# A linear-attention recurrence with a gated MLP: the cyclic timetable worked out anew, loads of the inner dense products twelve positions ahead

## The chip, the cores and the metric

The kernel runs on one core of a Trainium2 chip. The metric is device time in microseconds of one execution, from the core's own run. Three runs of the kernel before took 732.81, 734.06 and 735.11 us; the median is 734.06 us. The profiled execution, on which all rows below rest, took 736.0 us, of which 733.8 us lie between its first and last instruction.

## The reference

A recurrence over 768 time steps, for 4 batches and 8 heads of 40 values each, is followed by an MLP with spatial gating over the result. The code below is shortened; all of it is float32.

```
# attention: state is [B, H, 40, 40]
for t in range(768):
    y[t]  = einsum('bhd,bhde->bhe', r[t], state)
    Sa    = einsum('bhde,bhe->bhd', state, a[t])
    state = state * w[t][:, :, None, :] - einsum('bhd,bhe->bhde', Sa, b[t])
    state = state + einsum('bhd,bhe->bhde', v[t], k[t])
x = y as [4, 768, 320]
# MLP
h = gelu_tanh(x @ w_in)                       # 320 -> 1024
u, v = h[..., :512], h[..., 512:]
v_n  = (v - mean(v)) / sqrt(var(v) + 1e-6) * g_ln
v_s  = einsum('ts,bsd->btd', w_sg, v_n) + b_sg[None, :, None]
out  = x + (u * v_s) @ w_out                  # 512 -> 320
```

## The kernel before, in words

**Chunks.** The 768 steps are cut into 12 chunks of 64 (`C`, `NCH`), and each chunk into two halves f = 0 and f = 1 of two batches each. Within a chunk the recurrence becomes dense products; between chunks only the state is carried.

**Three kinds of work for a chunk.** (1) *Gates* (`gate_1` to `gate_n`, L303 to L378): scans over the decays on VectorE, products `ab` and transposes `kt` on TensorE; they need the tile `main` (642 KB a half chunk in two DMAs, two buffers) and run about four chunks ahead. (2) *Inverse* (`inv_sub`, L383): a triangular inverse for two chunks at a time, as 58 multiply and add instructions on GpSimd (POOL, tiles `tg` and `x`), turned by VectorE (`x1z`) and completed by the small products `gp` and `xp`. (3) *Chain* (`chain1` L464 to `post5` L585): the recurrence itself. For each half: `ru`, `us`, `ut`, `sp`, `pq`, `yp` on TensorE, and each one's result is taken out by ScalarE (`rhsb`, `vu`, `vut`) or VectorE (`pqs`, `yt`); `sp` gives the new state, copied to `vs` for the next chunk's `ru`; `tp` turns the state for `yp`, and ScalarE copies it to `s2` (shown as `s`; two buffers, L493). `post5` stores the half chunk's result `yt` to `xd` in DRAM, in four DMAs.

**Inner dense products ("fills").** While the recurrence runs, the first 640 of the 768 tokens of every batch are already taken through half of `x @ w_in`. There are 20 such fills, one for a batch and 128 tokens: `fill_x` loads `xf` from `xd` (three DMAs, L880), `fill_split` makes the rounded part `xfh` on ScalarE (L887), `fill_low` makes the rest `xfl` on POOL and stores both (L894), `fill_v` multiplies (`hf`, eight products, L904), `fill_out` copies `hf` to `hv` on ScalarE and stores it to `hd` (L912; `hv` has one buffer). The weights for this come in six stages `wstep` (L1044): load `stg`, ScalarE `size`, VectorE steps, ScalarE `wvh`, and a last step on VectorE, or on POOL in stages 1, 3 and 5. After the recurrence `run` (L1074) does the rest of the MLP.

**What sets the order.** There is no scheduler. Each piece of work is put into a list with a *position*, a number worked out by hand from tables (L42 to L88): `PER` is the number of positions from one chunk to the next, `YC` the position at which a chunk's chain begins, `GATE`, `CHAIN`, `FILL`, `INV`, `BACK` give each piece's distance from it. `in_order` (L98) sorts the list and holds pieces back where a PSUM bank is still taken in that order. Every instruction, DMAs too, is then issued in this order on its engine: all DMAs on one queue (SP), which stops at a DMA whose tile isn't free or whose source isn't there, with all later ones behind it. The code gives a position no unit.

**Lines that matter here.** The load of the next `main` stands in `gate_3`, straight behind the last reader (L333); the loads for the chain follow their last reader by 0.001 positions:

```
if i == 1:
    load_main(2 * c + f + 2)                                  # L333
at_(z + n[0] + 0.001, load_vb, c + 1, f)                      # L627
at_(z + max(n[6], n[9]) + 0.001, load_vu, c + 1, f)           # L628
at_(z + n[13] + 0.001, load_rv, c + 1, f)                     # L629
at(YC[min(2 * k + 2 + b // 2, NCH - 1)] + FEXTRA.get((b, k), 0) + p, f, b, k)   # L1050, fills
```

All instructions are issued by one helper (L172), so the profile shows that line for each, and the tiles' names tell them apart.

Of the kernel before, what the change touches and what calls it, by code (L numbers as in the profile page):

```python
# [18 lines left out]
NCH = S // C  # L19
# [17 lines left out]
WARM = 14  # L37
WARMS = ((-6.677, 8), (-6.177, 8))
BLANKS = -21.0
ZEROS = -36.0  # L40
LOADS = -24.0
PER = 26.5  # L42
GATE = ((-105.675, -104.069, -102.527, -98.826, -101.029, -97.64, -92.831, -91.094, -94.751, -92.741, -92.857),
    (-95.861, -93.341, -91.539, -89.807, -90.663, -89.233, -81.947, -80.028, -86.574, -83.227, -84.708))
CHAIN = ((0.0, 1.572, -9.235, -7.206, 2.08, 2.941, 4.523, 6.296, 11.564, 3.945, 4.686, 5.697, 7.113, 8.443, 10.749),
    (0.973, 2.583, 12.51, 15.829, 3.295, 5.224, 16.164, 18.719, 20.203, 6.977, 8.552, 10.046, 11.456, 17.819, 20.766))
YC = (0, 27.5, 80.0, 106.5, 133.0, 159.5, 186.0, 212.5, 239.0, 265.5, 292.0, 318.5)
YG = (39.675, 59.675, 80.0, 106.5, 133.0, 159.5, 186.0, 212.5, 239.0, 265.5, 292.0, 318.5)
YI = (-5.677, 21.823, 80.0, 133.0, 186.0, 239.0, 292.0)
GATEE = {(0, 0): "VG", (0, 1): "GG"}  # L50
GROUPS = ((0,), (1,), (2, 3), (4, 5), (6, 7), (8, 9), (10, 11))
LAST = 2
NBANK = 6
INV = (-63.232, -55.232, -53.032, 0.764, -8.432, -6.979)
INV1 = (-44.0, -29.3, -27.1, 0.429, -2.0, -1.3)
BACK = (-4.894, -2.14, -3.644, -5.677, -3.145, -1.402, 0.525)
END_GT = 238.772
END_IW = 285.071
END_RING = 286.366
END_IV = 319.525  # L60
CG = 0.7978845608028654
G1 = 0.044715
PIN = 238.782
DSTEP = ((-8.5, -1.0, 0.0, 0.7, 1.4, 2.4), (-8.5, -1.0, 0.0, 0.7, 1.4, 2.4))
DSTEPF = (-2.5, -0.5, 0.0, 0.7, 1.4, 2.4)
DEC = (5.0, 15.0, 25.0, 35.0, 45.0, 55.0, 247.782, 253.782, 259.782, 265.782, 271.782, 277.782)
GE = "VV"
FILL = ((-14.041, -8.441, -7.991, -4.381, -1.035), (3.788, 9.388, 9.838, 14.139, 17.326))
FEXTRA = {}
FILLG = True  # L70
LASTF = 5
PX = 319.725
PXS = 319.735
PV = 286.466
PS = 336.549
PL = 329.549
PF = (310.0, 315.0, 320.0, 325.0, 330.0)
PH = 9
# [7 lines left out]
SGS = (5, 3, 5, 6, 7, 8, 8, 11, 10, 11, 12, 11)  # L86
PO = 238.792
DECO = (283.782, 289.782, 295.782, 301.782, 307.782, 313.782, 319.782, 325.782)  # L88
DSTEPO = (-8.5, -1.0, 0.0, 0.7, 1.4, 2.4)
# [8 lines left out]
def in_order(pieces):  # L98
# [7 lines left out]
    def emit(x):  # L106
        nm = x[1].__name__
        if nm in USES and not (nm == "chain_t" and x[2][0] == 0 or nm == "chain3" and x[2][0] == NCH - 1):
            n, _, k = USES[nm]
            if any(left[b] for b in banks[max(0, len(banks) - NBANK):max(0, len(banks) + n - NBANK)]):  # L110
                return False
            left[key(x)] = k
            banks.extend([key(x)] * n)
        for r, n in ends:
            if nm == r and key(x, n) in left:
                left[key(x, n)] -= 1
        out.append(x)
        return True

    def behind(x):  # L120
# [3 lines left out]
        for h in held:  # L124
            hn = h[1].__name__
            if (nm, hn) in ends and key(x, hn) == key(h) or nm == "copy3" and hn == "post3" and x[2] == h[2]:
                return True
            if nm == "gate_3" and hn.startswith("gate") or nm.startswith("load_v") and hn.startswith("chain"):
                return True
# [56 lines left out]
def attention(tc, a, xd, flag, keep, ps, mlp=None):  # L186
# [4 lines left out]
    with ExitStack() as ctx:  # L191
# [32 lines left out]
        n = WU  # L224
# [78 lines left out]

        gate, kbs, unit, x1_of, st2, pqt, bk, xin = {}, {}, {}, {}, {}, {}, {}, {}

# [17 lines left out]
        def gate_3(c, f, i, E=V):  # L323
# [7 lines left out]
            E.tensor_tensor(out=kbs[c, f][:, i].rearrange("p q x t -> p x q t"), in0=kab[:, i, 0:3:2], in1=hv, op=ALU.mult)  # L331
            if i == 1:
                load_main(2 * c + f + 2)  # L333

# [275 lines left out]
        for c in range(NCH):  # L610
            for f in range(2):
# [9 lines left out]
                for h in range(2):  # L621
                    at_(y + n[9] + 0.001 * h, gate_a, c, f, h)
                    at_(y + n[10] + 0.001 * h, gate_n, c, f, h)
                z, n = YC[c], CHAIN[f]
                for g, p in zip((chain1, post1, chain_t, post_t, chain2, post2, chain3, post3, copy3, chain_u, post_u, chain4, post4, chain5, post5), n):
                    at_(z + p, g, c, f)
                at_(z + n[0] + 0.001, load_vb, c + 1, f)  # L627
                at_(z + max(n[6], n[9]) + 0.001, load_vu, c + 1, f)  # L628
                at_(z + n[13] + 0.001, load_rv, c + 1, f)  # L629
            z = YC[c]  # L630
# [44 lines left out]
class Mlp:  # L675
# [354 lines left out]
    def side(self):  # L1030
# [216 lines left out]
```

## Time and profile before

| | |
|---|---|
| median of three runs | 734.06 us |
| profiled execution | 736.0 us (span 733.8 us) |
| granted TensorE clock, mean | 0.841 |
| TensorE busy (products / weight loads) | 578.4 us (79%) / 525.2 us (72%) |
| VectorE, ScalarE, GpSimd busy | 485.6, 334.2, 354.3 us |
| DMA | 89.5 MB, mean 122 GB/s |
| first `ru` of chunks 0, 1, 2, 11 | 70.83, 109.30, 181.35, 473.6 us |
| last `yt` of the recurrence begins | 506.3 us |

The program has three stretches: gates and inverse of the first chunks until 70.8 us, the recurrence with its fills to about 507 us, and the MLP's rest. In the chunk-to-chunk stretch the chunk's start is read from the first product `ru` of half 0. A position and a microsecond can be compared there: from chunk 2 to chunk 11 the tables count 9 x 26.5 = 238.5 positions, and the profile 292.28 us.

### The profile page before, as it was taken

The numbers are of one execution on the slowest core, as the hardware profiler recorded it, in microseconds if no ns is written. First come the engines' busy times: TensorE is split into PE (matmuls) and PEld (weight loads), VectorE is DVE, ScalarE is ACT, GpSimd is POOL, SyncE is SP. The second block draws the span as 40 slices with busy tenths as digits, with TensorE's granted clock in tenths as the row PEclk, the third lists the DMA queues.
The fourth block names the chain that finished last, engine by engine and source line by source line (L and its number), as shares of the span: only waits on it lengthen the run. The fifth ranks groups of instructions, "written<-read, shape, count | busy, mean of one in ns | idle before, by whom it ended". The sixth has DMA issues, their size and how long they took to land.

```text
span 733.8 us, 25290 instructions
## 1 busy us (share of the span) xinstructions
PE 578.4 (79%) x10710; PEld 525.2 (72%) x10710; DVE 485.6 (66%) x950; ACT 334.2 (46%) x736; POOL 354.3 (48%) x596
## 2 busy tenths in 40 slices
PE   5474746626879799888987789759789998899996
PEld 4463646625768698777875578558679997799995
DVE  5864765876647674776758764345648979978942
ACT  2342444444555646466564645453424523444410
POOL 4386722785474358347836944123433423424331
PEclk8577866756889967799998877859899999999999
DMA  5470352533444645556455353654532275142001
GB/s 182 131 158 22 92 126 63 136 76 99 128 125 123 189 116 147 147 153 179 113 165 148 107 147 109 166 177 133 158 128 71 76 253 157 53 169 71 28 22 38
DMA packets 87138, 89.50 MB, mean 122 GB/s; under 512 B 38280, under 2 KB 69000, under 8 KB 85000
## 3 DMA queue, kind: packets, MB, share of 16 engines
q1 hardware_dynamic: 87016, 87.79, 42.2%
q8 instruction: 86, 1.41, 0.8%
q14 instruction: 36, 0.29, 0.1%
HBM read 68.10 MB, written 19.66 MB: 120 GB/s over the span
## 4 chain that ended last, share of the span: by engine, by line
PE 30%; DVE 18%; DMA 14%; ACT 7%; issue 6%; POOL 6%; SPq 4%; POOLq 0%; ACTq 0%; DVEq 0%
PE sg L172 8%; SPq L172 4%; PE ut L172 3%; PE yp L172 3%; PE op L172 3%; DVE v L172 3%; PE hf L172 2%; PE pq L172 2%; DVE p L172 2%; DMA hd<-hv 2%; POOL x L172 2%; DMA xf<-xd 2%; PE sp L172 2%; DVE g L172 2%; DMA rt<-rt 2%
## 5 line engine op out<-in xcount | busy, mean ns | idle before, releaser
L172 POOL TENSOR_TENSOR tg<-x,n 128x135 f32<-128x135 f32 (+25 forms) x203 | 104.5, 515 | 55.6 <-issue 15.5
L172 POOL TENSOR_TENSOR x<-x,tg 128x135 f32<-128x135 f32 (+25 forms) x203 | 108.7, 535 | 15.8
L172 PE MATMUL ab<-at,kb 64*64 64x64 f32 x1536 | 39.4, 261 | 48.8 <-DVE kb L172 20.9
L172 ACT ACTIVATE nts<-ab 32x512 f32<-32x512 f32 x96 | 46.5, 484 | 60.4 <-PE ab L172 59.2
L172 PEld LDWEIGHTS ab<-at,kb 64*64 64x64 f32 x1536 | 34.6, 172 | 53.8 <-DVE kb L172 23.7
L172 PE MATMUL sg<-wsl,vh 128*128 128x384 f32 x192 | 67.9, 354 | 5.5 <-POOL wsl L172 3.6
L172 PE MATMUL sg<-wsh,vh 128*128 128x384 f32 x192 | 67.6, 352 | 5.6 <-ACT wsh L172 3.3
L172 POOL TENSOR_TENSOR gx<-g,gy 128x384 fp32r<-128x384 f32 x32 | 34.1, 1070 | 74.0 <-ACT gy L172 74.0
L172 PE MATMUL sg<-wsh,vl 128*128 128x384 f32 x192 | 67.7, 352 | 0.9 <-POOL vl L172 0.9
L172 POOL TENSOR_TENSOR xfl<-xf,xfh 128x256 fp32r<-128x256 f32 x20 | 15.1, 757 | 83.8 <-ACT xfh L172 80.9
L172 POOL TENSOR_TENSOR rs<-rs,mhalf 128x1 f32<-128x1 f32 x24 | 14.9, 625 | 78.7 <-DVE rs L172 75.0
L172 DVE TENSOR_TENSOR at<-ab,mask 64x512 f32<-64x512 f32 x48 | 32.1, 677 | 27.8 <-ACT nts L172 18.2
L172 ACT CAST gy<-g 128x384 fp32r<-128x384 f32 x32 | 16.4, 513 | 62.9 <-DVE g L172 60.7
L172 PEld LDWEIGHTS sg<-wsl,vh 128*128 128x128 f32 x192 | 37.8, 197 | 7.7 <-POOL wsl L172 4.4
L172 PE MATMUL ut<-ident,vu 64*64 64x64 f32 x768 | 40.8, 257 | 2.6 <-ACT vu L172 2.2
L172 PEld LDWEIGHTS sg<-wsh,vh 128*128 128x128 f32 x192 | 38.0, 198 | 6.6 <-ACT wsh L172 3.9
L172 ACT CAST vh<-v 128x512 fp32r<-128x512 f32 x24 | 14.6, 619 | 60.3 <-DVE v L172 60.3
L172 PE MATMUL yp<-pqs,kbt 128*64 128x64 f32 x768 | 35.5, 253 | 8.0 <-DVE pqs L172 7.5
L172 PE MATMUL pq<-rt,vut 40*64 40x64 f32 x1536 | 38.5, 263 | 3.7 <-ACT vut L172 2.3
L172 PE MATMUL gp<-x1z,nts 64*32 64x32 f32 x768 | 18.2, 212 | 28.1 <-DVE x1z L172 27.2
L172 PEld LDWEIGHTS ut<-ident,vu 64*64 64x64 f32 x768 | 35.0, 167 | 6.5 <-ACT vu L172 3.5
L172 PEld LDWEIGHTS yp<-pqs,kbt 128*64 128x64 f32 x768 | 30.5, 162 | 12.7 <-DVE pqs L172 9.9
(154 smaller groups left out, 1589.3 us busy)
## 6 DMA issues: line engine op xcount, KB each, us to landing
main<-main SPq DMA_DIRECT2D x44, 321.4 KB
hd<-hv SPq DMA_DIRECT2D x20, 256.0 KB
v<-hd SPq DMA_DIRECT2D x20, 256.0 KB
vu<-vs SPq DMA_DIRECT2D x24, 160.0 KB
vs<-vb SPq DMA_DIRECT2D x24, 160.0 KB
rt<-rt SPq DMA_DIRECT2D x48, 80.0 KB
vut<-vt SPq DMA_DIRECT2D x48, 80.0 KB
xd<-yt SPq DMA_DIRECT2D x96, 40.0 KB
```

Source lines behind the costliest of these rows:

```text
L172: return self.tc.keep_in_program_order(f(*a, **k))
```

## The change

The tables are replaced. `PER` falls from 26.5 to 25.5. In `CHAIN` the two halves of a chunk, which began 0.97 positions apart, begin 11.0 apart, and most distances between a product and the instruction that takes its result become longer; half 1 of the last chunk ends at position 341.5 (339.3 before), half 0 at 330.2 (329.2 before). `load_main` and the chain's loads move 2.5 positions (`LATE`) behind the last reader, the store of `yt` becomes a piece of its own (`store5`) 1.5 positions (`STORE`) behind `post5`. In `FILL` the load of `xf` stands 12 positions ahead of its split (5.6 before), a fill's products come half a chunk or more later, and the two fills of a chunk end 13.8 and 11.7 positions apart (18.4 and 8.1 before). `in_order` takes the new pieces and the warm-up's bank into account. The kernel's arithmetic, tiles and sizes stay as they are. Two lines of the tables stand for all.

```
-PER = 26.5
+PER = 25.5
+LATE = 2.5
+STORE = 1.5
-CHAIN = ((0.0, 1.572, -9.235, -7.206, 2.08, 2.941, 4.523, 6.296, 11.564, 3.945, 4.686, 5.697, 7.113, 8.443, 10.749),
+CHAIN = ((0.0, 1.942, 2.468, 5.095, 5.152, 6.489, 14.151, 16.047, 17.757, 7.942, 9.521, 12.185, 14.84, 17.073,
...
-FILL = ((-14.041, -8.441, -7.991, -4.381, -1.035), (3.788, 9.388, 9.838, 14.139, 17.326))
+FILL = ((-9.701, 2.299, 2.749, 5.899, 8.777), (3.497, 15.497, 15.947, 19.922, 22.61))
...
+        if nm == "warmup":
+            left["wp"] = 0
+            banks.append("wp")
...
-            if nm == "gate_3" and hn.startswith("gate") or nm.startswith("load_v") and hn.startswith("chain"):
-                return True
+            if nm in ("gate_3", "load_main") and hn.startswith("gate"):
+                return True
+            if (nm.startswith(("load_v", "load_r")) or nm == "store5") and hn.startswith(("chain", "post")):
+                return True
...
-            if i == 1:
-                load_main(2 * c + f + 2)
...
+        def store5(c, f):
+            yt = yts[f]
             for i in range(2):
...
+                at_(y + n[5] + LATE, load_main, 2 * c + f + 2)
...
-                at_(z + n[0] + 0.001, load_vb, c + 1, f)
-                at_(z + max(n[6], n[9]) + 0.001, load_vu, c + 1, f)
-                at_(z + n[13] + 0.001, load_rv, c + 1, f)
+                at_(z + n[14] + STORE, store5, c, f)
+                at_(z + n[0] + LATE, load_vb, c + 1, f)
+                at_(z + max(n[6], n[9]) + LATE, load_vu, c + 1, f)
+                at_(z + n[13] + LATE, load_rv, c + 1, f)
...
-                for f, p in zip((self.fill_x, self.fill_split, self.fill_low, self.fill_v, self.fill_out), FILL[b % 2]):
-                    at(YC[min(2 * k + 2 + b // 2, NCH - 1)] + FEXTRA.get((b, k), 0) + p, f, b, k)
+                for f, p in zip((self.fill_x, self.fill_split, self.fill_low, self.fill_v, self.fill_out), FILL[1 - b % 2]):
+                    n = 2 * k + 2 + (b + 1) // 2
+                    at(YC[min(n, NCH - 1)] + PER * max(0, n - NCH + 1) + p, f, b, k)
```

**The DMA queue in a middle chunk.** SP's rows over most of a chunk before, for half 1 of one chunk (`main` is the gates' load, `xd<-yt` the store of the result, `xf`, `xhd`, `xld`, `hd` a fill's load and stores, the rest the chain's loads):

```order
L172 DMA xhd<-xfh 384x1x128
L172 DMA xld<-xfl 256x1x128
L172 DMA xd<-yt 40x4x64 x4
L172 DMA xf<-xd 128x2x128
L172 DMA xf<-xd 64x128 x2
L172 DMA vu_127<-vs 64x640
L172 DMA x<-x 128x1024
L172 DMA main_97<-main 40x2057 x2
L172 DMA hd<-hv 128x512
L172 DMA rt_122<-rt 40x512
```

The same queue after the change, from one fill's load to the other's:

```order
L179 DMA xf<-xd 128x2x128
L179 DMA xf<-xd 64x128 x2
L179 DMA rt_122<-rt 40x512
L179 DMA vut_125<-vt 40x8x64
L179 DMA rt_122<-rt 40x512
L179 DMA vut_125<-vt 40x8x64
L179 DMA xd<-yt 40x4x64 x4
L179 DMA hd<-hv 128x512
L179 DMA main_96<-main 40x2057 x2
L179 DMA vs_115<-vb 64x640
L179 DMA xf<-xd 128x2x128
L179 DMA xf<-xd 64x128 x2
```

Before, the `xf` of one of the chunk's two fills follows a store at once (1.7 positions by the tables; the other one's stands 9.5 behind a store), and this `hd` follows `main`. Now `hd`, `main` and `vs`, and 8.8 positions, stand between the store and the `xf` behind it (7.9 for the other fill's), and this `hd` stands ahead of `main`.

**The DMA queue in the first chunks.** SP before, around the loads of the weight stages 0 and 1 (`stg`):

```order
L172 DMA vs_115<-vb 64x640
L172 DMA stg_885<-w_in 128x512
L172 DMA vu_126<-vs 64x640
L172 DMA rt_121<-rt 40x512
L172 DMA vut_124<-vt 40x8x64
L172 DMA rt_121<-rt 40x512
L172 DMA vut_124<-vt 40x8x64
L172 DMA main_96<-main 40x2057 x2
L172 DMA xd<-yt 40x4x64 x4
L172 DMA stg_1171<-w_in 128x512
```

SP after the change, from the first load of `vs` on:

```order
L179 DMA vs_114<-vb 64x640
L179 DMA stg_837<-w_in 128x512
L179 DMA stg_993<-w_in 128x512
L179 DMA main_96<-main 40x2057 x2
L179 DMA vs_115<-vb 64x640
L179 DMA vu_126<-vs 64x640
```

Stage 1's load moves from behind `main` and a store to straight behind stage 0's.

**ScalarE around a chunk's start.** ScalarE before, from the end of one chunk into the next (`hv` and `xfh` are a fill's copies, `kbt` and `at` the gates', the rest the chain's):

```order
L172 COPY hv<-hf 128x512
L172 COPY kbt_111<-kt_3520 128x320
L172 COPY kbt_111<-kt_3521 128x320
L172 COPY xt_98<-xp 32x16x32 x2
L172 COPY rhsb_116<-ru 128x320
L172 COPY rhsb_117<-ru 128x320
L172 ACTIVATE vu_126<-us_3617 64x4x40 x2
```

ScalarE after the change, at the same chunk's start:

```order
L179 COPY vs_115<-sc_120 64x8x40 x2
L179 COPY rhsb_116<-ru 128x320
L179 CAST xfh<-xf 128x384
L179 COPY xt_98<-xp 32x16x32 x2
L179 COPY s_3570<-tp 104x320
L179 COPY s_3574<-tp 104x320
L179 COPY at_138<-at_138 64x8x64
L179 ACTIVATE vu_126<-us_3576 64x4x40 x2
L179 ACTIVATE vu_126<-us_3577 64x4x40 x2
L179 COPY hv<-hf 128x512
```

The copy `hv`, which stood just ahead of the chunk's start, now stands behind the first `vu`; half 1's `rhsb_117` is gone from here; a split `xfh` and the two copies of the turned state stand between `rhsb_116` and `vu_126`.

## Rows read from the trace of the kernel before

**Rows 1.** Busy time by engine in stretches of the span, granted clock, DMA.

```profile
core 0: us, PE busy (x) PEld busy (x) DVE busy (x) ACT busy (x) POOL busy (x), PEclk, DMA share, GB/s
70.83:109.30 38.47, 24.55 (x730) 22.00 (x724) 25.01 (x51) 17.81 (x40) 19.78 (x48) 0.73 0.39 102
109.30:181.35 72.05, 41.39 (x952) 37.22 (x948) 47.60 (x95) 30.83 (x69) 43.02 (x75) 0.62 0.38 96
181.35:473.63 292.28, 246.95 (x6842) 216.28 (x6844) 185.78 (x361) 164.61 (x375) 162.44 (x278) 0.86 0.51 140
473.63:507.07 33.44, 23.01 (x485) 21.22 (x485) 14.91 (x39) 14.30 (x35) 8.72 (x16) 0.74 0.50 153
507.07:733.80 226.73, 205.10 (x1100) 195.25 (x1098) 167.19 (x321) 82.98 (x169) 80.07 (x79) 0.97 0.33 103
218.57:248.88 30.31, 25.21 (x813) 22.38 (x809) 22.94 (x41) 17.70 (x39) 11.42 (x23) 1.00 0.52 144
248.88:280.65 31.77, 30.46 (x810) 27.68 (x809) 19.82 (x39) 18.71 (x42) 19.69 (x34) 0.79 0.56 149
251.00:254.00 3.00, 1.75 (x68) 1.40 (x68) 1.26 (x2) 2.45 (x7) 2.58 (x6) 1.00 0.73 213
257.00:260.00 3.00, 3.00 (x90) 2.92 (x90) 1.88 (x4) 0.71 (x2) 0.00 (x0) 0.50 0.20 60
```

**Rows 2.** The chain that ended last, 286 to 320 us: start, us, what.

```profile
294.71 6.75 DMA main<-main
...
301.47 3.73 DMA xd<-yt
...
309.33 7.15 DMA hd<-hv
```

**Rows 3.** Timeline 286 to 350 us; brackets: idle before, releaser.

```profile
304.22 1.15 PE L172 MATMUL yp<-pqs,kbt 128*64 128x64 f32 x32
...
305.25 1.65 SPq L172 DMA_DIRECT2D xf<-xd  x3
...
305.30 0.66 PE L172 MATMUL yp<-rt,s 40*40 40x64 f32 x32
...
309.37 0.51 ACT L172 CAST xfh<-xf 128x384 fp32r<-128x384 f32 x1 [5.35 <-DMA xf<-xd]
...
309.96 0.73 POOL L172 TENSOR_TENSOR xfl<-xf,xfh 128x256 fp32r<-128x256 f32 x1 [9.16 <-ACT xfh L172]
```

**Rows 4.** Waits from 181.35 to 473.63 us: total, times, longest.

```profile
POOL xfl L172 <- ACT xfh L172: 80.9, 15, 9.2
ACT xfh L172 <- DMA xf<-xd: 34.3, 8, 5.7
...
ACT hv L172 <- DMA hd<-hv: 2.8, 3, 1.4
```

**Rows 5.** Waits of the DMA queue SP, the same stretch.

```profile
SPq L172 <- DVE kb L172: 20.1, 6, 4.2
SPq L172 <- PE yp L172: 19.9, 7, 6.7
```

**Rows 6.** Timeline of the first chunks, 84 to 135 us.

```profile
87.10 1.40 SPq L172 DMA_DIRECT2D main<-main  x2
...
90.20 0.39 SPq L172 DMA_DIRECT2D stg<-w_in  x1
...
98.72 0.72 POOL L172 TENSOR_TENSOR stg<-stg,stg 128x256 f32<-128x256 f32 x1 [8.94 <-ACT wvh L172]
...
124.18 0.53 SPq L172 DMA_DIRECT2D stg<-w_in  x1
...
131.26 0.73 POOL L172 TENSOR_TENSOR stg<-stg,stg 128x256 f32<-128x256 f32 x1 [15.60 <-ACT wvh L172]
```

**Rows 7.** Timeline of the last chunk, 470 to 512 us.

```profile
482.37 1.95 PE L172 MATMUL us<-rhsb,xt 64*64 64x40 f32 x64 [6.73 <-ACT rhsb L172]
...
506.26 0.76 DVE L172 TENSOR_TENSOR yt<-yp,ex 128x256 f32<-128x256 f32 x2
```

More of the change, by code (lines that the diff above doesn't have):

```diff
@@ L37 @@
 WARM = 14
-WARMS = ((-6.677, 8), (-6.177, 8))
+WARMS = ((-4.831, 8), (-4.331, 8))
 BLANKS = -21.0
@@ L41 @@
 LOADS = -24.0
-PER = 26.5
-GATE = ((-105.675, -104.069, -102.527, -98.826, -101.029, -97.64, -92.831, -91.094, -94.751, -92.741, -92.857),
-    (-95.861, -93.341, -91.539, -89.807, -90.663, -89.233, -81.947, -80.028, -86.574, -83.227, -84.708))
-CHAIN = ((0.0, 1.572, -9.235, -7.206, 2.08, 2.941, 4.523, 6.296, 11.564, 3.945, 4.686, 5.697, 7.113, 8.443, 10.749),
[L46 to L49, printed above, removed]
+PER = 25.5
+LATE = 2.5
+STORE = 1.5
+GATE = ((-101.908, -100.107, -99.028, -96.184, -97.801, -95.604, -92.188, -90.251, -93.577, -91.478, -91.823),
+    (-93.163, -92.271, -89.673, -85.987, -88.462, -85.151, -80.147, -78.616, -83.325, -79.712, -81.287))
+CHAIN = ((0.0, 1.942, 2.468, 5.095, 5.152, 6.489, 14.151, 16.047, 17.757, 7.942, 9.521, 12.185, 14.84, 17.073,
+    19.654), (11.001, 12.574, 2.94, 4.267, 13.405, 14.279, 15.32, 18.186, 26.426, 16.496, 19.044, 24.204, 26.192,
+    29.01, 31.005))
+YC = (0, 27.5, 81.0, 106.5, 132.0, 157.5, 183.0, 208.5, 234.0, 259.5, 285.0, 310.5)
+YG = (35.908, 55.908, 81.0, 106.5, 132.0, 157.5, 183.0, 208.5, 234.0, 259.5, 285.0, 310.5)
+YI = (-3.831, 23.669, 81.0, 132.0, 183.0, 234.0, 285.0)
 GATEE = {(0, 0): "VG", (0, 1): "GG"}
@@ L53 @@
 NBANK = 6
-INV = (-63.232, -55.232, -53.032, 0.764, -8.432, -6.979)
+INV = (-61.011, -53.011, -50.811, 0.759, -6.51, -5.143)
 INV1 = (-44.0, -29.3, -27.1, 0.429, -2.0, -1.3)
[L56 to L60, printed above, removed]
+BACK = (-3.831, -0.954, -1.454, -2.595, -0.449, 1.071, 3.249)
+END_GT = 232.184
+END_IW = 279.907
+END_RING = 292.105
+END_IV = 314.249
 CG = 0.7978845608028654
 G1 = 0.044715
-PIN = 238.782
+PIN = 232.194
 DSTEP = ((-8.5, -1.0, 0.0, 0.7, 1.4, 2.4), (-8.5, -1.0, 0.0, 0.7, 1.4, 2.4))
 DSTEPF = (-2.5, -0.5, 0.0, 0.7, 1.4, 2.4)
-DEC = (5.0, 15.0, 25.0, 35.0, 45.0, 55.0, 247.782, 253.782, 259.782, 265.782, 271.782, 277.782)
+DEC = (5.0, 15.0, 25.0, 35.0, 45.0, 55.0, 241.194, 247.194, 253.194, 259.194, 265.194, 271.194)
 GE = "VV"
-FILL = ((-14.041, -8.441, -7.991, -4.381, -1.035), (3.788, 9.388, 9.838, 14.139, 17.326))
-FEXTRA = {}
+FILL = ((-9.701, 2.299, 2.749, 5.899, 8.777), (3.497, 15.497, 15.947, 19.922, 22.61))
 FILLG = True
 LASTF = 5
[L72 to L77, printed above, removed]
+PX = 314.449
+PXS = 314.459
+PV = 292.205
+PS = 338.954
+PL = 331.954
+PF = (303.0, 308.0, 313.0, 318.0, 323.0)
 PH = 9
@@ L86 @@
 SGS = (5, 3, 5, 6, 7, 8, 8, 11, 10, 11, 12, 11)
-PO = 238.792
-DECO = (283.782, 289.782, 295.782, 301.782, 307.782, 313.782, 319.782, 325.782)
+PO = 232.204
+DECO = (277.194, 283.194, 289.194, 295.194, 301.194, 307.194, 313.194, 319.194)
 DSTEPO = (-8.5, -1.0, 0.0, 0.7, 1.4, 2.4)
@@ L302, in nt_of @@
             return nts[c // 2 % 2][:, c % 2]
-        gate, kbs, unit, x1_of, st2, pqt, bk, xin = {}, {}, {}, {}, {}, {}, {}, {}
+        gate, kbs, unit, x1_of, st2, pqt, bk, xin, yts = {}, {}, {}, {}, {}, {}, {}, {}, {}
         def gate_1(c, f, i):
@@ L590, in post5 @@
                                 in1=exs[ent(c, f)][:, :, x:NP:2, 0:C], op=ALU.mult)
+            yts[f] = yt
+        def store5(c, f):
+            yt = yts[f]
             for i in range(2):
```

## The prediction, made before the changed kernel was run

> **What bounds the kernel now.** I first cut the span at the first `ru` of chunks 0, 1, 2 and 11 and asked for the busy time in each stretch [rows 1]. The reader is to see that no engine is full before 507 us. From chunk 2 to chunk 11, 292.28 us or 32.5 us a chunk, TensorE's products are busy 246.95 us, so 45.3 us are idle; VectorE (185.8), ScalarE (164.6) and POOL (162.4) have much more room. In the MLP's rest products fill 205.10 of 226.73 us, and no instruction is changed there. In the middle stretch the tables count 26.5 positions for what takes 32.5 us, and most of the prediction is about that difference.
>
> Second, the chain that ended last, in one chunk's turn [rows 2]: `main` 6.75 us, the store `xd` 3.73 us, then `hd` from 309.33 us on for 7.15 us: 17.6 us of a chunk of 35.5 us are transfers. The timeline has what lies between [rows 3]: SP stands until the store has landed, issues `xf` at 305.25 us, ScalarE stands idle 5.35 us for it until 309.37, and POOL, whose next instruction is that fill's `xfl`, 9.16 us. Third, the waits over the whole stretch say how often [rows 4]: ScalarE waits 34.3 us for `xf`, 8 times in 9 chunks (one of the two fills of a chunk, the one whose load follows a store at once), and POOL 80.9 us for `xfh`. ScalarE works in order, so behind `xfh` stand the gates' `nts` and `kbt`, and the next chunk's `rhsb`, for which `us` waits. Last, SP's own waits [rows 5]: it stands 20.1 us for `kb` because `load_main` is queued with its last reader, and 19.9 us for `yp`.
>
> The clock comes on top. Where the products are busy only 1.75 of 3 us at a chunk's start (251 to 254 us), the granted clock is still 1.00; at 257 to 260 us it is 0.50, the lower level of 1.2 GHz, with the products busy throughout [rows 1]. The same products of a chunk take 25.21 us busy at 1.00 and 30.46 us at 0.79 [rows 1]: 0.25 us for each hundredth of clock. At the mean of 0.86, fourteen hundredths cost 3.5 us a chunk, 31 us over nine chunks.
>
> **The change, part by part.** All sums stand against the profiled execution's 736.0 us (733.8 us span and 2.2 us around it); the median of the runs is 1.9 us lower, which comes off at the end.
>
> *Middle, loads and fills.* All distances are those of the tables. `xf` is issued 12 positions ahead of its split, at 32.5/26.5 = 1.23 us each 14.7 us, where store and load together need 3.73 us and about 4 us (305.25 to 309.37) [rows 2, 3]; even behind a whole `main` that is 14.5 us. Two `hd` stand at least 11.7 positions apart against 7.15 us for one. `main` is issued 16.7 and 15.0 positions (18 us) ahead of its first reader against 6.75 us; the chain's loads are issued 2.5 positions later than before and keep 18 or more. If that cover went, each would cost what `main` costs, 6.75 us a time. No DMA is added; the four of a store move past `main` or a fill's two, and SP reaches each DMA after its source is done, so most of the 40.0 us of [rows 5] should go.
>
> *Middle, what is late next.* TensorE itself, with the same products in its own order. It can't get all 45.3 us, since each chunk still has the serial chain product, copy, product. The trace shows no such timetable, so I bound it. Upper end: all idle and all lost clock returned, 45.3 + 31 = 76 us. Lower end: nothing, or a loss, by the one wait that the change adds. `s2` has two buffers; the copy `s` of half 1 now stands 0.76 positions behind the `yp` that still reads the buffer, before it stood 24.5 behind. The `yp` products take 1.15 + 0.66 = 1.8 us [rows 3], so ScalarE can stand about 1 to 1.8 us a chunk, and behind it the other `s`, `at`, and `vu`, for which `ut` waits: 9 x 1.8 = 16 us at worst. I take 40% of the idle time, 18 us, as the transfers are the larger part of the chain's turn but the product's copies stay; and a quarter of the clock, 8 us, as one of the chunk's low stretches begins with a stall that should shrink. Middle: -26 us, a chunk of 29.6 us (between -76 and +16).
>
> One rule weighs on this size. Products leave 45.3 us of the stretch free, weight loads 292.28 - 216.28 = 76.0 us [rows 1]. The Trainium skill (Perfetto Trace Analysis, "Identifying the Most-Contended Engine") says that busy time of products misjudges TensorE's headroom, and that the weight loads' share is the better measure; by it 40% would be 30 us, and the middle -38. I keep the products, because with the products at 3.00 of 3 us the weight loads already fill 2.92 [rows 1].
>
> *First chunks.* POOL's inverse of chunk 1 stops 8.94 us for weight stage 1, whose load SP issues at 90.20 us, behind `main` at 87.10; the inverse of chunks 2 and 3 stops 15.60 us for stage 3, loaded only at 124.18 us, because SP stood behind a load waiting for `sp` [rows 6]. These stops lie on the path: chunk 1 and chunk 2 begin when the inverse is done. Stage 1's load now stands straight behind stage 0's, and stage 3's no longer behind that load. Against it the inverse starts 2 to 3 positions later, and stage 5 still stands behind `main`. Of 24.5 us I take 9 (between -20 and +6, the later start with nothing gained).
>
> *Last chunk.* It takes 33.4 us to the last `yt` (473.6 to 507.0) for 20.8 positions [rows 1, 7], 1.6 us each, with ScalarE held by weight stages and gelus for its first part (`us` waits 6.73 us) [rows 7]. Half 1 now ends 31 positions after the chunk's start. The added 10.2 positions cost between 10.2 x 1.6 = 16 and -2 us, should the first part run without its stops. I take +8: beyond position 13 little else stands in the way. The last fill's eight products move behind the recurrence's end; they only change places on TensorE, up to 2 us.
>
> *The rest*: 0 (between -3 and +3), the same instructions.
>
> Sum: 736.0 - 9 - 26 + 8 = 709.0 us; less 1.9 us, **707 us**.
>
> **The rivals.**
>
> *Full relief.* With no stall at the chunk's start the clock stays high. First chunks -15, middle 60% of 76 us = -46, end +6: 736.0 - 55 - 1.9 = 679 us. For it: the low clock begins right after the stall [rows 1]. Against it: products as fully busy as in the chunk from 248.88 to 280.65 us, 30.46 of 31.77, still ran at 0.79 for the whole. The Trainium skill (TensorE: Matmul & The Clock Gate, "HAM oscillation — how this bites in real kernels") has a clock that falls after every wait for a transfer and comes back where the waits go; by it this is the case to expect, and the row at 251 to 254 us agrees with its first half.
>
> *TensorE is the next bound.* The waits go, but the products take their place at the present clock: a quarter of the idle time, 11 us, no clock, first chunks -5, end +8: 736.0 - 8 - 1.9 = 726 us. For it: 30.46 of 31.77 us are filled in one chunk already [rows 1].
>
> *The lag of half 1 is paid and not earned back: slower.* Place: the last chunk, where nothing runs beside half 1's last 10.2 positions, +16 us. In the middle the wait for `s2` takes what the loads gave, -4, first chunks 0: 736.0 + 12 - 1.9 = 746 us. It decides as soon as first chunks and middle give less than 16 us, under 1.5 us a chunk. For it: by the tables the new end, 341.5, is not earlier than the old, 339.3; all the gain has to come from waits that the tables don't know. Against it: 17.6 us of transfers in one turn of the chain [rows 2].
>
> *The loads don't come earlier in fact*: SP is in order, and an earlier position doesn't issue `xf` earlier if SP is held by something else; then waits move and the sum is about 0, 734 us.
>
> **How the numbers follow.** Forecast 707 us: 0.45 (its own range 697 to 718). TensorE next, 726: 0.20. Full relief, 679: 0.13. Slower, 746: 0.16. No effect, 734: 0.06. A measurement of this kernel tells 0.3%, about 2 us, from no change. Faster by more: 0.45 + 0.20 + 0.13, 0.78; within: 0.06; slower: 0.16. The range of 8 in 10 holds forecast, TensorE next and no effect (0.71) and the nearer parts of the two outer cases: 682 to 738 us.
>
> **What would show it.** Right: from chunk 2 to chunk 11 about 266 us, ScalarE's wait for `xf` near nothing and POOL's for `xfh` under 30 us, no `hv` waiting for `hd`; POOL's two stops in the first chunks under half; the last chunk near 41 us. Wrong in its main step: these waits gone and the chunk still over 31 us, which is TensorE or its clock; or ScalarE's `s` waiting over 1 us in each chunk. Wrong altogether: a chunk of 32 us with the last one over 45 us.

## The result, and the profile after

The changed kernel takes 699.72 us (median of four runs, 691.79 to 702.58) where the kernel before took 733.43 us (four runs, 729.50 to 735.11). The ratio is 0.951, interval 0.942 to 0.961: faster by 3.9 to 5.8%. The profiled execution took 702.58 us, its span 700.5 us; before, 736.0 and 733.8. Stretches and waits are read from one profiled run of each kernel, which can lie well off the median of its runs: 2.9 us above it for the changed kernel, and in the experiments below 10.9 us below it for e4, 6.7 above for e10 and 13.0 below for e12.

The windows of the changed kernel, cut at the first `ru` of chunks 0, 1, 2 and 11 and at the last `yt`, columns as in [rows 1]:

```profile
71.90:110.70 38.80, 26.02 (x710) 23.84 (x702) 29.00 (x62) 21.19 (x49) 21.14 (x49) 0.68 0.41 112
110.70:174.00 63.30, 37.02 (x969) 33.07 (x968) 44.20 (x88) 28.12 (x64) 39.53 (x64) 0.69 0.38 98
174.00:433.70 259.70, 226.22 (x6772) 200.84 (x6768) 184.53 (x358) 164.21 (x372) 161.26 (x282) 0.92 0.57 151
433.70:475.40 41.70, 29.79 (x613) 24.94 (x612) 19.77 (x46) 18.16 (x43) 12.59 (x22) 0.75 0.60 178
```

Beside [rows 1]: chunk 0 to 1 takes 38.8 us (38.5 before), chunk 1 to 2 63.3 (72.05), chunk 2 to 11 259.7 (292.28), the last chunk to the last `yt` 41.7 (33.44); 1.1 us are lost ahead of chunk 0, 1.6 gained behind the last `yt`. In the middle TensorE's idle time falls from 45.3 to 33.5 us, and its busy time from 246.95 to 226.22 us, at a mean granted clock of 0.92 instead of 0.86. The products are not quite the same: 72 fewer begin in this stretch than before, 64 `yp` (half 1 of chunk 10, which now ends in the last chunk) and the eight `hf` of one fill. By the rows of the chain below (64 `yp` 1.67 us, eight `hf` 2.05 us, both where the clock is 1.00) they are worth 3.7 us. So of 32.6 us only 11.8 are waiting time, some 3.7 are work that has moved into the last chunk, and about 17 are left for products that run faster; the last two are estimates. From chunk 2 to the last `yt`, where this move cancels for the `yp`, the time falls by 24.3 us (325.72 to 301.4).

The waits of the middle, beside [rows 4], then those of SyncE (SP in the rows), beside [rows 5] (total, times, longest):

```profile
POOL xfl L179 <- ACT xfh L179: 28.3, 11, 4.8
...
ACT s L179 <- PE yp L179: 10.3, 8, 2.6
```

```profile
SPq L179 <- PE ru L179: 21.3, 5, 9.7
...
SPq L179 <- PE yp L179: 2.8, 3, 1.6
SPq L179 <- DVE kb L179: 2.6, 1, 2.6
```

ScalarE's waits for `xf` (34.3 us) and for `hd` (2.8 us) have no row any more. POOL's wait for `xfh` fell from 80.9 to 28.3 us, SyncE's for `kb` and `yp` from 40.0 to 5.4 us; its wait for `ru` rose from 8.2 to 21.3. New is ScalarE's `s`, 1.3 us each of 8 times.

In the first chunks, 71.9 to 174 us, beside [rows 6], POOL still stands for weight stages, three times, and ScalarE for their loads:

```profile
POOL stg L179 <- ACT wvh L179: 15.9, 3, 8.1
...
ACT stg L179 <- DMA stg<-w: 14.5, 2, 8.1
```

The chain that ended last, in the turn of chunk 5 (start, us, what), beside [rows 2]:

```profile
263.04 1.06 PE ru L179 x32
...
266.26 1.67 PE yp L179 x64
267.93 0.45 PE us L179 x32
268.37 2.05 PE hf L179 x8
270.42 0.90 PE ut L179 x26
...
281.76 3.81 issue
285.57 1.77 PE ab L179 x56
287.35 3.71 PE hf L179 x8
```

Before, 17.6 us of one turn were transfers. Now no piece from 262 to 322 us is one: TensorE follows on TensorE, with one long gap of 3.81 us, for which the profile names no releaser, and one of 1.31 us at 313.26. The eight `hf` products take 2.05 us before that gap and 3.71 us behind it. The windows of this stretch say why:

```profile
261.90:281.90 20.00, 19.74 (x676) 17.73 (x672) 15.54 (x31) 15.25 (x35) 15.29 (x27) 1.00 0.58 155
281.90:285.60 3.70, 0.03 (x4) 0.03 (x4) 3.50 (x8) 0.00 (x0) 0.14 (x1) 0.80 1.02 260
285.60:291.10 5.50, 5.50 (x66) 4.50 (x67) 2.86 (x4) 1.93 (x4) 0.00 (x0) 0.51 0.65 178
291.10:313.30 22.20, 21.43 (x698) 19.04 (x696) 16.16 (x32) 17.12 (x38) 13.67 (x27) 1.00 0.61 158
```

The clock is at its upper level, 2.4 GHz, up to the gap, and near the lower one, 0.51, for the 5.5 us behind it.

### The profile page after: what moved, and what is told of

Same layout as the page of the kernel before. It is cut to its first block, busy times and chain, and to the rows that moved or that the text cites. A ratio compares the mean times of both kernels' runs of the same rounds, so it can differ in the third digit from the quotient of the medians.

```text
span 700.5 us, 25303 instructions
## 1 busy us (share of the span) xinstructions
PE 558.7 (80%) x10710; PEld 509.5 (73%) x10710; DVE 486.9 (70%) x950; ACT 336.1 (48%) x736; POOL 351.9 (50%) x596
## 4 chain that ended last, share of the span: by engine, by line
PE 44%; DVE 16%; issue 6%; ACT 4%; POOL 2%; DMA 2%; SPq 1%; POOLq 0%; ACTq 0%; DVEq 0%
PE sg L179 10%; PE hf L179 5%; PE yp L179 5%; PE op L179 3%; PE ru L179 3%; DVE v L179 3%; PE ut L179 3%; PE pq L179 3%; PE sp L179 2%; DVE p L179 2%; PE ab L179 2%; DVE cv L179 2%; PE xp L179 2%; DVE g L179 2%; PE kt L179 2%
## 5 line engine op out<-in xcount | busy, mean ns | idle before, releaser
L179 POOL TENSOR_TENSOR x<-x,tg 128x135 f32<-128x135 f32 (+25 forms) x203 | 106.1, 523 | 15.8
L179 PE MATMUL ab<-at,kb 64*64 64x64 f32 x1536 | 42.4, 268 | 56.3 <-DVE fixed L179 22.7
L179 PEld LDWEIGHTS ab<-at,kb 64*64 64x64 f32 x1536 | 36.9, 175 | 61.0 <-issue 31.8
L179 DVE TENSOR_TENSOR pqs<-pq,mask 128x512 f32<-128x512 f32 x48 | 30.7, 681 | 14.5 <-PE pq L179 14.5
L179 DVE TENSOR_TENSOR yt<-yp,ex 128x256 f32<-128x256 f32 x48 | 18.1, 417 | 31.5 <-PE yp L179 30.2
L179 PEld LDWEIGHTS sg<-wsh,vl 128*128 128x128 f32 x192 | 37.3, 194 | 2.1 <-POOL vl L179 2.0
L179 PE MATMUL kt<-ident,kb 128*128 128x128 f32 x192 | 35.2, 342 | 2.8 <-issue 2.8
L179 PE MATMUL ut<-ident,vu 64*64 64x64 f32 x768 | 32.2, 235 | 6.1 <-ACT vu L179 6.1
L179 PEld LDWEIGHTS ut<-ident,vu 64*64 64x64 f32 x768 | 28.1, 146 | 11.3 <-ACT vu L179 8.7
L179 POOL TENSOR_TENSOR vl<-v,vh 128x512 fp32r<-128x512 f32 x24 | 31.6, 1320 | 8.8 <-ACT vh L179 8.8
```

Source lines behind the costliest of these rows:

```text
L179: return self.tc.keep_in_program_order(f(*a, **k))
```

## The experiments

Three parts can be had or left out apart from each other: the new *timetable* of the recurrence (`CHAIN`, `GATE`, `YC` and what follows from them), the *lead* of the loads of `xf` (12 positions instead of 5.6), and the *spread* (`LATE`, `STORE`). On the old timetable the lead does not come alone: the new `FILL` also puts a fill's products half a chunk later, so e1 and e4 differ from the kernel before in both. The first table has what was measured for their combinations. The stretches are those of one profiled run each, in us: chunk 0 to 2, chunk 2 to 11, chunk 11 to the first `hu`; the clock is that of chunk 2 to 11.

| kernel | timetable | lead | spread | ratio to before, interval | 0 to 2 | 2 to 11 | 11 to `hu` | clock |
|---|---|---|---|---|---|---|---|---|
| before | old | 5.6 | no | 1 | 110.5 | 292.3 | 29.2 | 0.86 |
| e1 | old | 12 | no | 0.988, 0.981 to 0.995 | 106.0 | 284.7 | 38.1 | 0.87 |
| e4 | old | 12 | yes | 0.983, 0.973 to 0.994 | 104.4 | 277.1 | 36.9 | 0.89 |
| e2 | new | 5.6 | no | 1.002, 0.996 to 1.008 | 114.1 | 273.7 | 48.4 | 0.90 |
| e5 | new | 5.6 | yes | 0.999, 0.996 to 1.002 | 102.1 | 281.1 | 46.8 | 0.90 |
| e3 | new | 12 | no | 0.973, 0.967 to 0.979 | 115.3 | 256.3 | 42.2 | 0.90 |
| changed | new | 12 | yes | 0.951, 0.942 to 0.961 | 102.1 | 259.7 | 41.2 | 0.92 |

Runs of one kernel lie up to 2.6% apart (before, 722 to 741 us on one chip), and kernels that differ outside the middle alone (changed, e7, e8) have middles between 257 and 260 us, so 3 us of difference there say nothing. Against the kernel before, the middle holds eight `hf` fewer in e1 and e4, and these and 64 `yp` fewer in the kernels with the new timetable.

**Loads alone (e1).** The old tables, no spread, and

```
-FILL = ((-14.041, -8.441, ...), (3.788, 9.388, ...))
+FILL = ((-9.701, 2.299, ...), (3.497, 15.497, ...))
```

> The old timetable of the recurrence, with the new positions of the fills alone: the load of xf twelve positions ahead of its products, and the products half a chunk later. The spread of the loads and of the store by 2.5 and 1.5 positions is left out. If the gain comes from transfers that are no longer waited for (theory A, the one behind my forecast), most of the middle's gain is here: ScalarE's wait for xf (34 us before) and GpSimd's wait for xfh (81 us) fall, chunk 2 to 11 comes down from 292 to about 272 us, and the time is about 712 us. If the gain comes from the new distances between a product and the copy behind it (theory B), the wait for xf goes but other waits take its place, and the time is 726 to 734 us. If TensorE's granted clock carries it (theory C), the time falls only as far as the clock in the middle rises from 0.86.

Measured: 728.5 us (726.68 to 740.03). By theory A most of the middle's gain had to be here; 7.6 of 32.6 us are. The rows of the middle that say why, of before and then of e1 (waits, as above):

```profile
ACT vut L172 <- PE ut L172: 25.3, 17, 3.1
...
DVE sp L172 <- PE sp L172: 16.0, 6, 4.0
```

```profile
ACT vut L178 <- PE ut L178: 44.0, 18, 5.6
POOL xfl L178 <- ACT xfh L178: 31.1, 8, 7.7
...
DVE sp L178 <- PE sp L178: 24.9, 7, 6.5
```

The wait for `xf` is gone, and ScalarE stands for the products `ut` instead, 18.7 us more than before, VectorE 8.9 us more for `sp`. That is theory B's outcome in kind, with a small gain. The time line of e1 shows what makes the wait for `ut` longer (start, us, what):

```profile
270.19 1.25 ACT L178 ACTIVATE vu<-us 64x160 f32<-64x160 f32 x4
...
272.23 0.97 PE L178 MATMUL hf<-wvh,xfh 128*128 128x512 f32 x3
...
274.28 1.15 PE L178 MATMUL ut<-ident,vu 64*64 64x64 f32 x32
...
275.47 0.59 ACT L178 COPY vut<-ut 104x512 f32<-104x512 f32 x1 [3.52 <-PE ut L178]
```

`vu` is there at 271.44, but TensorE has a fill's eight products `hf` to do before `ut`. With TensorE's and ScalarE's rows laid over each other, TensorE is busy with `hf` in 17.8 of the 44.0 us of waiting, in the kernel before in none of the 25.3. So nearly the whole rise comes from the products' new place, which the same edit gave them. In the changed kernel eight `hf` also stand ahead of a `ut`, but there they run while ScalarE still makes `vu`: from 268.30 to 270.42 us, `vu` from 268.98 to 270.22. Outside the middle e1 gains 4.5 us up to chunk 2 and loses 8.9 between chunk 11 and `hu`.

**Timetable alone (e2).** The changed kernel with `LATE = 0.001`, `STORE = 0.0005` and the loads 5.6 positions ahead.

> The new timetable of the recurrence (half 1 eleven positions behind half 0, a chunk each 25.5 positions), with the loads of xf 5.6 positions ahead as they were before and with no spread of the loads and the store. The products of the fills stand half a chunk later, as in the changed kernel. Theory A: ScalarE again waits for xf about 3 to 4 us per fill, and the time is 722 to 730 us. Theory B: the time is 703 to 712 us, nearly all of the gain. Theory C: the clock in the middle tells which of the two it is, 0.86 with A and 0.92 with B.

Measured: 738.76 us (736.95 to 739.37), no difference to before. Theory B falls, and A does not fit either: the middle gets 18.6 us shorter and the clock 0.90, but the first chunks lose 3.6 us and the last 19.2. `vut`'s wait has gone to 5.7 us, and the transfers stand in its place:

```profile
POOL xfl L179 <- ACT xfh L179: 43.9, 13, 6.8
ACT xfh L179 <- DMA xf<-xd: 42.5, 14, 6.7
...
ACT vut L179 <- PE ut L179: 5.7, 9, 1.2
```

So each part alone has its own wait: the new timetable without the lead keeps the one for `xf`, and the new loads and fills without the timetable put `hf` in the way of `ut`.

**Both, without the spread (e3).** The changed kernel with `LATE = 0.001`, `STORE = 0.0005`.

> The changed kernel without the spread: loads and the store are issued right behind the piece that frees their buffer, so that they stand at the head of SyncE's queue and block it until that piece is done, as before. Theory A in its form for the queue (SyncE held by a load that waits holds up all loads behind it): SyncE's waits for kb and yp (20 us each before, 3 us each after) come back, the loads of xf come later, and the time is 708 to 716 us. Theory B: 699 to 703 us, no difference to the changed kernel.

Measured: 716.79 us (715.27 to 718.29), just past theory A's upper end, but not for A's reason. The middle is not longer (256.3 us); SyncE's waits for `kb` and `yp` do not come back there. Between the two profiled runs, 12.7 us apart, all of the difference is in the first two chunks, 115.3 us instead of 102.1; the medians are 17.1 us apart.

**Lead and spread on the old timetable (e4).** The old tables with the new `FILL`, `LATE` and `STORE`, and with `PL`, the position of one load of `xt`, moved from 329.549 to 331.3, so that it follows the later store.

> The old timetable of the recurrence with both parts that are about transfers: loads of xf twelve positions ahead, and the spread of the other loads and of the store. Theory A: nearly the whole gain of the middle, 703 to 710 us; what stays is the shorter period. Theory B: 726 to 734 us. The difference between this run and the one with the old timetable and the new fills alone is the price of the blocked queue: by theory A 3 to 10 us, by theory B 0.

Measured: 731.48 us (720.56 to 735.26), ratio 0.983. A falls, B's 726 to 734 holds for the time. Against e1 the spread adds nothing that the intervals can tell.

**The lead taken back from the changed kernel (e5).**

```
-FILL = ((-9.701, 2.299, ...), (3.497, 15.497, ...))
+FILL = ((-3.3, 2.299, ...), (9.898, 15.497, ...))
```

> The changed kernel with the spread and all else, but the load of xf only 5.6 positions ahead of its split, as before the change. What the four runs so far say: the timetable without lead and spread took 273.7 us from chunk 2 to 11, with the lead 256.3. Theory A (the lead is worth what ScalarE's wait for xf costs): that wait is back at some 3 us a fill, chunk 2 to 11 takes 272 to 278 us instead of 260, and the time is 712 to 720 us. Theory B (with the spread SyncE is free and the load is in time even so): 700 to 704 us.

Measured: 730.44 us (ten runs, 726.74 to 734.57). A is right in kind, and its price was too small: the whole gain is gone. The wait for `xf` is higher than in the kernel before:

```profile
ACT xfh L179 <- DMA xf<-xd: 54.5, 13, 8.2
...
POOL xfl L179 <- ACT xfh L179: 51.3, 14, 6.0
```

On the old timetable the lead, with the products' new places, is worth 1.2%; on the new one 3% without the spread (e2, e3) and 5% with it (e5, changed).

**The spread, by place (e6, e9).** In e6 `LATE` and `STORE` are used for pieces with c < 2 alone, in e9 `LATE` for `load_main` alone:

```
-                at_(y + n[5] + LATE, load_main, 2 * c + f + 2)
+                at_(y + n[5] + LATEC(c), load_main, 2 * c + f + 2)
```

where `LATEC(c)` is `LATE` for c < 2 and 0.001 otherwise; and of e9, for each of the chain's loads and in the same way for the store:

```
-                at_(z + n[0] + LATE, load_vb, c + 1, f)
+                at_(z + n[0] + 0.001, load_vb, c + 1, f)
```

> The changed kernel with the spread of loads and store in chunks 0 and 1 alone; from chunk 2 on they are issued right behind the piece that frees their buffer. Without any spread the first two chunks took 115.3 us instead of 102.1, and the middle 256.3 instead of 259.7. Theory A (the spread pays because weight loads stand behind a blocked SyncE, which is a thing of the first chunks alone): 699 to 704 us, the first two chunks at 100 to 104 us and the middle unchanged. Theory B (it pays throughout): 706 to 714 us.

> The changed kernel with the spread for load_main alone; the chain's three loads and the store are issued right behind the piece that frees their buffer. The run with the spread for chunks 0 and 1 left out the main loads that are issued during the first chunks, since these belong to the gates of later chunks, and the first two chunks kept 112.4 us. Theory A (SyncE stands with a main load that waits for kb, and the weight loads stand behind it): 698 to 704 us, the first two chunks 100 to 104 us. Theory B (the chain's loads and the store block it): 712 to 718 us, the first two chunks 112 us or more.

Measured: e6 715.17 us (713.84 to 717.72), e9 709.33 us (707.92 to 710.32). Neither theory holds whole in either: e6 is 1 us past B's upper end, with its middle unchanged (258.2 us), as A has it; e9 lies between the two. By stretches the four runs fall apart cleanly. In e6 the chain's loads and the stores of the first chunks are spread, but not the `main` loads issued there, which belong to the gates of later chunks; in e9 it is the other way round.

| | chunk 0 to 1 | chunk 1 to 2 |
|---|---|---|
| e3, no spread | 47.8 | 67.5 |
| e6, chain's loads and store | 48.5 | 63.9 |
| e9, `main` | 38.8 | 68.0 |
| changed, both | 38.8 | 63.3 |

The spread of `main` takes 9 us off the first stretch, that of the others 4 us off the second. What `main` does there is to be seen in SyncE's wait for `kb` in chunk 0 to 1, in its issues on the timeline and in ScalarE's first step on each weight stage (`stg<-stg`; start, us, what), first of e3:

```profile
SPq L179 <- DVE kb L179: 12.1, 1, 12.1
```

```profile
86.51 0.66 SPq L179 DMA_DIRECT2D main<-main  x2
...
87.79 1.51 SPq L179 DMA_DIRECT2D stg<-w_in  x1
...
95.74 0.43 ACT L179 ACTIVATE stg<-stg 128x256 f32<-128x256 f32 x1 [5.72 <-DMA stg<-w_in]
...
107.22 0.69 SPq L179 DMA_DIRECT2D main<-main  x2
...
107.99 0.35 SPq L179 DMA_DIRECT2D stg<-w  x1
```

and then of e9:

```profile
SPq L179 <- DVE kb L179: 0.8, 1, 0.8
```

```profile
85.38 0.53 SPq L179 DMA_DIRECT2D stg<-w_in  x1
...
86.76 0.68 SPq L179 DMA_DIRECT2D main<-main  x2
...
90.31 0.45 ACT L179 ACTIVATE stg<-stg 128x256 f32<-128x256 f32 x1
...
101.80 0.37 SPq L179 DMA_DIRECT2D stg<-w  x1
...
102.26 0.69 SPq L179 DMA_DIRECT2D main<-main  x2
```

Without the spread SyncE stands 12.1 us, until 86.51, with a `main` load whose buffer `kb` still reads, and weight stage 1's load stands behind it. With the spread this weight load goes first, 2.4 us earlier, and ScalarE has its data 5.4 us earlier (90.31 instead of 95.74). The same 5.4 us are found again at the store ahead of stage 2's load (issued at 99.64 instead of 105.06), and that load too now stands ahead of its `main`: it is issued 6.2 us earlier, and ScalarE's first step on stage 2 comes at 107.14 instead of 115.85 us.

**More room for the weight stages (e7).**

```
-DSTEPF = (-2.5, -0.5, 0.0, 0.7, 1.4, 2.4)
+DSTEPF = (-8.5, -0.5, 0.0, 0.7, 1.4, 2.4)
-            return self.fl.tile([128, n], dt, name=f"stg{n}", tag=f"w{n}", bufs=HF // n)
+            return self.fl.tile([128, n], dt, name=f"stg{n}", tag=f"w{n}", bufs=2)
```

and `bufs=2` for `hv`, which shares the tag.

> The changed kernel with a second buffer for the stage of the weights (and for hv, which shares it), and each weight load issued 8.5 positions ahead of its first reader instead of 2.5. In the changed kernel's first chunks ScalarE still waits 14.5 us for such loads and GpSimd 15.9 us behind it. Theory A (these stops lie on the way to chunks 1 and 2): chunk 0 to 2 takes 88 to 97 us instead of 102.1, the time is 687 to 697 us. Theory B (the inverse of the first chunks has its own length and the stops only fill gaps): 102 us and 699 to 703 us.

Measured: 693.59 us (688.02 to 697.29), ratio 0.942, interval 0.932 to 0.952; chunk 0 to 2 95.6 us. That is A, at its weak end: chunk 0 to 2 is 6.5 us shorter, where ScalarE stood 14.5 us for the loads and POOL 15.9 us behind it.

**Less lag at the end (e8).** For c = 11, f = 1 all positions of `CHAIN` but those of `chain_t` and `post_t` are lowered by 5.

> The changed kernel, in which the last chunk's half 1 runs five positions earlier (but for tp and s); all else is the same. My forecast put the last chunk's +8 us on the ten positions by which half 1 ends later. Theory A (so it is): taking half of the lag back gives 4 to 5 us, the last chunk takes 36 to 38 us instead of 41.7 and the time is 695 to 697 us. Theory B (the first product hu waits for half 0's own way: yt, its store, the load of xt and the split, while ScalarE is held by weight stages and gelus): the last chunk keeps 41 to 43 us, the time stays at 699 to 702 us.

Measured: 700.52 us (695.41 to 702.49), theory B by the time. The last `yt` comes 38.7 us after the chunk's start instead of 41.7, between the two theories, but the first `hu` only 1 us earlier, 40.2 instead of 41.2. What stands ahead of `hu` is half 0's way, here in the changed kernel, beside [rows 7] (timeline; brackets: idle before, releaser):

```profile
445.19 0.43 PE L179 MATMUL us<-rhsb,xt 64*64 64x40 f32 x2 [5.84 <-ACT xt L179]
...
465.52 0.76 DVE L179 TENSOR_TENSOR yt<-yp,ex 128x256 f32<-128x256 f32 x2 [6.72 <-PE yp L179]
...
468.31 2.04 SPq L179 DMA_DIRECT2D xt<-xd  x4
...
472.94 0.96 PE L179 MATMUL hf<-wvh,xfh 128*128 128x512 f32 x3
...
473.35 0.51 ACT L179 CAST xh<-xt 128x384 fp32r<-128x384 f32 x1 [3.35 <-DMA xt<-xd]
...
474.35 0.29 DVE L179 TENSOR_TENSOR xh<-xt,xh 64x128 fp32r<-64x128 f32 x1
...
474.67 0.76 DVE L179 TENSOR_TENSOR yt<-yp,ex 128x256 f32<-128x256 f32 x2
...
474.90 0.69 PE L179 MATMUL hu<-xh,wuh 128*128 128x384 f32 x3
```

Half 0's `us` waits 5.84 us for `xt`, a copy that belongs to the inverse. Its `yt` begins 31.8 us after the chunk's start and `hu` 9.4 us behind it; in between lie its store, the load of `xt` and the split, and `hu` follows the split by 0.3 us. Half 1's last `yt` falls in beside it. But the last fill's eight `hf` also stand ahead of `hu` in TensorE's order and are done only when it begins. In e8 the split is done at 472.12 us and `hu` comes at 472.76, behind these products; in e1, where half 0 has its old positions, the split is done at 489.93 and `hu` comes at 499.32, behind the last fill's `hf`. So the two ways to `hu` are not told apart: no run moves the last fill alone.

**The fill's products out of the way, old timetable (e10).** e1 with

```
-FILL = ((-9.701, 2.299, 2.749, 5.899, 8.777), ...)
+FILL = ((-9.701, 2.299, 2.749, 9.2, 12.0), ...)
```

> The run with the old timetable and the new loads alone, and one edit: the eight products of each chunk's first fill, and the copy behind them, stand 3.3 positions later, behind half 1's ut instead of between pq of half 0 and this ut. In that run ScalarE's wait for xf was gone, and its wait for ut rose from 25.3 to 44.0 us in the middle. Theory A (the fill's products stood on the recurrence's way on TensorE, and took the place of the wait for xf): the wait for ut falls under 25 us, chunk 2 to 11 comes from 284.7 to 265 to 275 us, and the time to 710 to 720 us. Theory B (the old timetable is too tight in itself, the wait moves to the next copy): 280 to 288 us, 724 to 731 us.

Measured: 737.53 us (731.89 to 744.21), ratio 1.014, interval 1.005 to 1.023, slower than e1. Neither theory holds. Only where it waits is read from the profile: ScalarE's wait for `ut` is down to 27.2 us, near the 25.3 of the kernel before, so the rise in e1 did come from the place of the `hf`. But 24.1 us of waiting for the products `hf` and 23.7 us of VectorE's for `pq` have come up. The wait moved on, at a loss.

**A third `s2` (e11).** `bufs=3` instead of 2 for `s2`.

> The changed kernel with a third buffer for s2, so that half 1's copy s needn't wait for the products yp that still read the buffer. In the changed kernel ScalarE waits 10.3 us for them in the middle, 8 times; my forecast put a price of up to 16 us on it. Theory A (it delays the copies behind it and so the recurrence): the middle gets 6 to 10 us shorter, 691 to 696 us. Theory B (ScalarE has room there; the wait costs nothing): 698 to 703 us.

Measured: 699.49 us (697.22 to 703.36). ScalarE's wait for `yp` is gone; the middle of the profiled run, 253.4 us, is 6.3 us shorter, as A has it, but the time is the changed kernel's, as B has it. Its ratio, 0.965 (0.957 to 0.973), is against runs on another chip, where before reached 722.44 us. Whether the wait costs anything stays open; a price of 6 us the times do not bear out.

**Together (e12).** e7 and e8, with

```
-DECO = (277.194, 283.194, ..., 319.194)
+DECO = (277.2, 281.8, ..., 309.4)
-DSTEPO = (-8.5, -1.0, ...)
+DSTEPO = (-6.0, -1.0, ...)
-PF = (303.0, 308.0, 313.0, 318.0, 323.0)
+PF = (299.5, 303.5, 307.5, 311.5, 315.5)
```

and `PH = 7`.

> A kernel meant to be faster: the changed kernel with the second buffer and earlier loads for the weight stages (693.6 us by itself), half 1 of the last chunk five positions earlier, and less for ScalarE and VectorE to do in the last chunk: the weight stages of w_out 4.6 positions apart instead of 6, and the first five gelus 3.5 to 7.5 positions earlier. Theory A (half 0's way through the last chunk is held up by ScalarE's weight stages and gelus): the last chunk takes 32 to 37 us instead of 41, the time is 686 to 691 us. Theory B (that work only moves into chunk 10 and takes there what it gives): 692 to 697 us.

Measured: 698.05 us (six runs, 685.04 to 700.35), ratio 0.961, interval 0.955 to 0.968. In the profiled run chunk 0 to 2 takes 90.4 us and the last chunk 38.2 to the first `hu` and 36.8 to the last `yt`, on either side of A's upper end. The median is past B's upper end. So a gain over the changed kernel is not shown, for e12 or for e7: their intervals and the changed kernel's overlap.

## Why the prediction was right, and where it was not

The forecast was 707 us, with a range of its own from 697 to 718; 699.72 lies in it. Three of the four terms came out near their size, but two of them for other reasons than those given. In the middle, idle time gave less than was priced and the clock more; that the two made up for each other in part is luck. The scatter was taken too small: 0.3% was allowed for, and runs of the kernel before lie up to 2.6% apart.

*Middle, -26; measured -32.6.* The mechanism was seen in part. The waits for `xf`, `hd`, `kb` and `yp` went as said, and TensorE is late next as said. The step that failed is the split, 18 us from idle time, put on the loads, and 8 us from the clock: it was 11.8 from idle time and about 17 from the clock, and some 3.7 are products that left the stretch. And the loads alone do not give 18: with them alone the idle time of the middle fell by 3.1 us (45.3 to 284.7 - 242.53 = 42.2), since the products that move with the loads came to stand ahead of `ut` (e1). The sum of waits at one engine was taken as a price, without asking what the same edit puts in the way elsewhere. The table shows two parts that need each other: in the middle the lead gives 7.6 us, the timetable 18.6, both together 36, and in the whole time 1.2%, nothing, and 2.7%. Whether the lead on the old timetable would give more with the products left in their places stays open, as no run has that.

*Clock, a quarter of what was lost; it was about half* (some 17 of 31 us; by the forecast's own price, 0.25 us a chunk for each hundredth, six hundredths are 13.5). It was taken for a consequence of fewer stalls. e5 speaks against that: it has 281.1 - 234.58 = 46.5 us idle, as much as before, and 0.90 all the same. Its busy time is 12.4 us less, of which the 72 products that left are some 3.7. e3, with the same timetable and products as e5, has only 26.7 us idle and 0.90 as well. The gain in clock goes with the new timetable, whatever the idle time's sum: the ten profiled runs with it have 0.90 to 0.92 in the middle, three of the four with the old one 0.86 to 0.89 and the fourth, e10, 0.85. Why is not settled. The Trainium skill (TensorE: Matmul & The Clock Gate, "HAM oscillation — how this bites in real kernels") has a clock that falls behind waits for a transfer. The row behind the 3.7 us gap agrees in that the clock fell behind a stall, though the profile names no transfer for it; that the sum of the stalls gives the mean clock, e3 and e5 do not bear out. Full relief, 679 us, did not come.

By the weight loads' share, the rule that was set aside, the middle would have been -38; measured is -32.6, halfway between the two. Both rules take 40% of TensorE's free time, 18 and 30 us; without products it fell by 11.8 us (26%), without weight loads by 17.1 (76.0 to 58.9, 23%). The share was too high by either, and no run here tells one measure from the other.

*The wait for `s2`* came as priced, 1.3 us a time, 8 times (1 to 1.8 a chunk foreseen). The forecast named a wait of over 1 us in each chunk as a sign that its main step is wrong. The sign came, but that the wait costs that much on the path is not borne out (e11).

*First chunks, -9; measured -8.4 between chunks 0 and 2.* The reason given was POOL's two stops, which were to fall under half of 24.5 us. POOL still stands three times, 15.9 us in all, longest 8.1: not under half. The runs put it differently: the new timetable without the spread costs 3.6 to 4.8 us here (e2, e3), and the spread gives 13.2. That a `main` load blocks a weight load was named in the forecast; that the new timetable makes it worse was not.

*Last chunk, +8; measured +8.3 (33.44 to 41.7), but not for half 1 alone.* The forecast put it on half 1's ten later positions. The last `yt` does follow them: with five taken back it came 3 us earlier (e8). But `hu` came only 1 us earlier and the time stayed. Half 0 now stretches over 19.7 positions of the last chunk where it took 10.7, and the first `hu` needs half 0's output; the last fill's products stand ahead of `hu` as well. TensorE is also busy 6.8 us more in this stretch (23.01 to 29.79), partly with the products that left the middle. Which of these sets the 12.0 us by which `hu` comes later (29.2 to 41.2) stays open: e1 has 8.9 of them with half 0's positions as before.

*The rivals.* "Loads don't come earlier" fell at once, since `xf` is no longer waited for. "TensorE next" is true of the chain, and its 11 us of idle time are what was measured (11.8); it is wrong in price, as the clock rose too. "The lag is paid and not earned back" is not what happened to this change, but it is what e2 shows: without the lead the new timetable gains 18.6 us in the middle and loses 22.8 outside it.

## What to carry to other kernels

Before a wait is priced, look at what else the same edit moves. Here the edit that brought the loads earlier also moved the products, and on the old timetable these stood in the way of `ut`. So two parts of a change can be worth little one by one and much together, and each is to be priced with the other in place. On an in-order DMA queue, do not put a load right behind the instruction that frees its buffer when other loads queue behind it: 2.5 positions of distance gave 13 us in the first two chunks, where weight loads stood behind `main`, and nothing that can be told in the middle. For an end term, follow back from the first instruction that comes after, not from the last one of the stage.

## What was not expected of the hardware

The granted clock of a stretch did not follow the sum of its idle time: from chunk 2 to 11 it was 0.90 at 26.7 us idle (e3) and 0.90 at 46.5 (e5), with the same products, and 0.86 at 45.3 in the kernel before, with another order of the work. Each is one profiled run, and the mean clock of whole runs of one kernel differs by up to 0.03 on one chip (0.816 to 0.848, the kernel before), so the step from 0.86 to 0.90 rests on ten profiled runs with the new timetable and four with the old one, and its cause is open.
